# ScalarE in pairs of banks with one VectorE tile beside, accumulators drawn from the free banks, a multiply moved to GpSimd, a late choice of shift engine

## The chip, the cores and the metric

One core of one Trainium2 chip runs the whole program. The metric is the device time of one execution in microseconds (us), taken in several rounds on one chip beside the kernel before. The ratios below use runs not over 1.5% above the fastest run of the same kernel. The engines are TensorE (PE; its weight loads are PEld), ScalarE (ACT), VectorE (DVE), GpSimd (POOL) and the DMA queue of SyncE (SP).

Each run also reports the mean clock granted to TensorE, as a share of full speed.

## The reference

Two independent blocks work on 2048 rows of 512 numbers; their outputs lie side by side.

```python
def _A_ref(x, wq, wk, wv, wo):            # 32 query heads of 16, one key and value head
    q = (x @ wq)...                       # [1, 32, 2048, 16]
    k, v = x @ wk, x @ wv
    scores = einsum("bhqd,bkd->bhqk", q, k) * (Dh ** -0.5)
    p = _softmax(scores, axis=-1)         # 32 x 2048 x 2048 exponentials
    o = einsum("bhqk,bkd->bhqd", p, v)
    return o... @ wo

def _B_ref(x, wqkv, w_phi, wo):           # linear attention, softmax features
    ...                                   # little work beside A
```

Block A's 134 million exponentials are the bulk of the work. Block B is some projections, 64 exponentials of 128 x 512 and many small steps, woven in between.

## The kernel before: the parts that matter

**Tiles and units.** Scores are made in tiles of 128 keys by 512 queries, 2048 of them. They are grouped in 32 accumulators ("sc"), each of 64 tiles, that is 16 quads of four tiles (one for each of TensorE's four row strips). A score tile fills one PSUM bank; the kernel lays PSUM out as eight banks of 128 x 512. A quad goes one of two ways:

- *ScalarE's way:* exponentiate from PSUM into a ring in SBUF, two or three banks per instruction; then TensorE multiplies by the values (`pv`, one turn for the quad).
- *VectorE's way:* turn the scores into the bit pattern of an approximate exponential (`dz`, one instruction a tile), make three shifted copies of the quad in SBUF (`dS`, on VectorE or POOL), and sum four weighted versions on TensorE (`dpv`, four turns for the quad).

**Banks before.** Five banks serve ScalarE (three and two, in turn), bank 5 is the accumulator, banks 6 and 7 serve everything else: VectorE's score tiles, all projections and all of block B.

```python
self.ACC = 5
self.free = [6, 7]
...
def next_qk(self, i):
    us = []
    for _ in range(3 if i % 2 == 0 else 2):
        u = self.take()
        ...
    n0, b0 = self.nu, 0 if i % 2 == 0 else 3
```

**One accumulator.** The next accumulator may not begin until the copy of the last one has been put in VectorE's queue:

```python
def acc_ok(self, sc):
    return self.acc_sc == sc              # set to None at an accumulator's end,
                                          # to sc + 1 when its copy is issued
```

**The finish of an accumulator** is a copy out of PSUM (`ac`), DMAs that spread the denominators, and a multiply of two SBUF tiles of 128 x 512 (`on`), all on VectorE except for the DMAs:

```python
self.add("dve", lambda v: v.tensor_tensor(out=o, in0=accS[:, r, :], in1=R[:, r, :], op=ALU.mult), ...)
```

**A planner orders everything.** While the kernel is built, a greedy planner keeps a clock for each engine from estimated durations, asks which jobs are ready, and issues the most urgent one. What it fixes is the order of each engine's instructions and how many tiles take VectorE's way. `LOCK` names the VectorE jobs that it never places beside a POOL instruction. It also puts in dummy matmuls ("fills") where its plan has TensorE idle for long; they are meant to keep TensorE's clock up.

## Time and profile before

| | kernel before |
|---|---|
| median of 4 runs | 747.89 us (747.03 to 748.63) |
| ScalarE tiles / VectorE tiles | 1512 / 536 |
| busy in the profiled run: ScalarE, VectorE, POOL | 724.5, 663.8, 371.7 us of 748.5 |
| shifts on VectorE / POOL | 219 / 183 |

The profiled run is not one of these four: it took 750.37 us. These are lines of the page of the kernel before: the span, the busy time of each engine (with its share of the span and its instructions), the lines of the chain that ended last, and the costliest groups. A group's columns are line, engine, operation, output and input with shapes, count; then busy us and mean ns; then the engine's idle time just before these instructions and what ended it.

```profile
span 748.5 us, 17531 instructions
PE 717.5 (96%) x7364; PEld 229.7 (31%) x7364; DVE 663.8 (89%) x1104; ACT 724.5 (97%) x676; POOL 371.7 (50%) x262
...
ACT 53%; PE 34%; DVE 10%; DMA 1%; issue 1%; ACTq 0%; DVEq 0%
...
L1641 ACT ACTIVATE f_PT<-f_ps 128x1536 bf16<-128x1536 f32 x605 | 696.4, 1298 | 14.2 <-PE f_ps L1586 13.1
L1769 POOL TENSOR_TENSOR f_Z<-f_Z,f_step 128x1024 int32<-128x1024 int32 x183 | 346.1, 1891 | 334.3 <-DVE f_Z L1764 329.1
L1738 DVE TENSOR_SCALAR f_Z<-f_ps 128x512 int16<-128x512 f32 x536 | 349.4, 681 | 36.3 <-PE f_ps L1586 33.9
L1586 PE MATMUL f_ps<-f_QA,f_KR 32*128 32x512 bf16 x2048 | 316.5, 386 | 17.3 <-ACT f_PT L1641 6.6
...
L1764 DVE TENSOR_SCALAR f_Z<-f_Z 128x2048 int16<-128x2048 int16 x219 | 149.2, 701 | 0.6
...
L1405 PE MATMUL f_ps<-f_ones,f_zero 128*32 128x512 bf16 (+8 forms) x264 | 49.2, 375 | 1.9 <-POOL f_zero L1424 1.3
```

How to read it. ScalarE is busy 97% and its exponentials (the first group) are the largest share of the chain: the time is, nearly, ScalarE's work. TensorE's 96% says less: 49.2 us are fills (the last line), and the Trainium skill ("Perfetto Trace Analysis", Identifying the Most-Contended Engine) warns that matmul busy time does not tell how close TensorE is to its limit. VectorE's tiles (`f_Z<-f_ps`) waited 33.9 us for a score matmul.

The same kernel's groups with shapes kept apart show the two widths and the multiply:

```profile
L1641 ACT ACTIVATE f_PT<-f_ps 128x1536 bf16<-128x1536 f32 x302 | 455.9, 1509 | 13.0 <-PE f_ps L1586 12.3
L1641 ACT ACTIVATE f_PT<-f_ps 128x1024 bf16<-128x1024 f32 x303 | 329.2, 1087 | 1.2 <-PE f_ps L1586 0.8
...
L1874 DVE TENSOR_TENSOR f_On<-f_accS,f_denS 128x512 bf16<-128x512 f32 x16 | 12.8, 797 | 4.3 <-DMA f_denS<-f_denS 4.3
...
L1874 DVE TENSOR_TENSOR f_Ot<-f_accS,f_denS 128x512 bf16<-128x512 f32 x15 | 10.6, 708 | 0.0
```

The means (1509, 1087 ns) overlap one another, so the price is read from start to start in the trace: 1.330 us for three banks when nothing delays the next, 0.904 us for two. I call a start that comes over 25 ns later than that *late*; before, 94 starts are late, by 20.0 us together.

### The profile page before, as it was taken

Reading aid. Unit: us, or ns where it says so; the run is one execution under the profiler, and the core shown is the slowest. Engines: PE = TensorE matmul, PEld = TensorE weight load, DVE = VectorE, ACT = ScalarE, POOL = GpSimd, SP = SyncE. Lnnn points to the kernel's source line nnn. Section 1 sums busy time; section 2 is a strip of 40 time slices with the busy share of each in tenths; the row PEclk is TensorE's granted clock in tenths of the full one; section 3 lists DMA queues with packets and bytes.
Section 4 is the critical chain, followed back from the end, with each engine's and each line's share of the span. In section 5 each row is a group of like instructions: output and inputs, shape, how many; then the busy total and the mean of one; then the engine's idle time right before and its main releaser. Section 6 shows DMA issues by size and latency. Waiting matters only on the chain.

```text
span 748.5 us, 17531 instructions
## 1 busy us (share of the span) xinstructions
PE 717.5 (96%) x7364; PEld 229.7 (31%) x7364; DVE 663.8 (89%) x1104; ACT 724.5 (97%) x676; POOL 371.7 (50%) x262
## 2 busy tenths in 40 slices
PE   8999999999999999989999999999999999999995
PEld 3323233233322323322232333233333333323321
DVE  4999998998998999998869999889998897999992
ACT  5999999999999999998999999999999999999995
POOL 4344466556555554345564454446545754553452
PEclk9999999999999999999999999999999999999999
DMA  6521223111102111011101112101111111111112
GB/s 142 115 37 8 37 36 75 9 11 10 10 6 36 12 9 9 7 8 9 12 4 10 29 23 27 9 2 27 19 16 9 23 33 26 16 9 20 19 16 40
DMA packets 47887, 18.25 MB, mean 24 GB/s; under 512 B 38708, under 2 KB 45940, under 8 KB 47800
## 3 DMA queue, kind: packets, MB, share of 16 engines
q1 hardware_dynamic: 45400, 16.23, 16.7%
q8 instruction: 59, 0.97, 0.5%
q10 hardware_dynamic: 2400, 0.82, 0.5%
q14 instruction: 28, 0.23, 0.1%
HBM read 2.28 MB, written 4.19 MB: 9 GB/s over the span
## 4 chain that ended last, share of the span: by engine, by line
ACT 53%; PE 34%; DVE 10%; DMA 1%; issue 1%; ACTq 0%; DVEq 0%
ACT f_PT L1641 51%; PE f_ps L1586 12%; PE f_ps L1806 9%; PE f_ps L1682 5%; DVE f_Z L1738 4%; ACT f_Ek L2059 2%; DVE f_Z L1764 2%; PE f_ps L2241 1%; PE f_ps L1405 1%; PE f_ps L1893 1%; PE f_ps L2149 1%; ACT f_ET L2156 1%; PE f_ps L1576 1%; DMA f_AxT<-in_A_x_dram 1%; PE f_ps L2225 1%
## 5 line engine op out<-in xcount | busy, mean ns | idle before, releaser
L1641 ACT ACTIVATE f_PT<-f_ps 128x1536 bf16<-128x1536 f32 x605 | 696.4, 1298 | 14.2 <-PE f_ps L1586 13.1
L1769 POOL TENSOR_TENSOR f_Z<-f_Z,f_step 128x1024 int32<-128x1024 int32 x183 | 346.1, 1891 | 334.3 <-DVE f_Z L1764 329.1
L1738 DVE TENSOR_SCALAR f_Z<-f_ps 128x512 int16<-128x512 f32 x536 | 349.4, 681 | 36.3 <-PE f_ps L1586 33.9
L1586 PE MATMUL f_ps<-f_QA,f_KR 32*128 32x512 bf16 x2048 | 316.5, 386 | 17.3 <-ACT f_PT L1641 6.6
L1806 PE MATMUL f_ps<-f_Z,f_VK 128*32 128x512 f16 x2144 | 189.7, 389 | 3.0 <-DVE f_accS L1411 1.3
L1586 PEld LDWEIGHTS f_ps<-f_QA,f_KR 32*128 32x128 bf16 x2048 | 82.2, 91 | 249.2 <-ACT f_PT L1641 133.1
L1764 DVE TENSOR_SCALAR f_Z<-f_Z 128x2048 int16<-128x2048 int16 x219 | 149.2, 701 | 0.6
L1682 PE MATMUL f_ps<-f_PT,f_VA 128*32 128x512 bf16 x1512 | 149.3, 388 | 0.2
L1806 PEld LDWEIGHTS f_ps<-f_Z,f_VK 128*32 128x32 bf16 x2144 | 48.6, 94 | 97.5 <-issue 62.6
L1682 PEld LDWEIGHTS f_ps<-f_PT,f_VA 128*32 128x32 bf16 x1512 | 38.6, 94 | 69.1 <-issue 62.7
L1405 PE MATMUL f_ps<-f_ones,f_zero 128*32 128x512 bf16 (+8 forms) x264 | 49.2, 375 | 1.9 <-POOL f_zero L1424 1.3
L2211 DVE TENSOR_TENSOR f_Wk<-f_ps,f_wq 128x512 bf16<-128x512 f32 x32 | 21.9, 685 | 2.5 <-PE f_ps L2200 2.3
L2065 DVE TENSOR_REDUCE f_ssum<-f_Ek 128x64 f32<-128x1024 bf16 x16 | 19.4, 1215 | 2.5 <-ACT f_Ek L2059 2.5
L1411 DVE COPY f_accS<-f_ps 128x512 f32<-128x512 f32 x31 | 21.1, 681 | 0.6 <-PE f_ps L1682 0.6
L1405 PEld LDWEIGHTS f_ps<-f_ones,f_zero 128*32 128x32 bf16 (+2 forms) x264 | 13.4, 98 | 24.2 <-issue 17.3
L2099 DVE TENSOR_TENSOR f_vS<-f_ps,f_rs 128x1024 bf16<-128x1024 f32 x16 | 19.5, 1221 | 1.4 <-PE f_ps L2089 1.3
L2156 ACT ACTIVATE f_ET<-f_ps 128x512 bf16<-128x512 f32 x32 | 19.1, 709 | 0.0
L2059 ACT ACTIVATE f_Ek<-f_ps 128x512 bf16<-128x512 f32 x32 | 18.7, 682 | 0.0
L2051 PE MATMUL f_ps<-f_Wk,f_BxT 128*128 128x512 bf16 x64 | 16.6, 382 | 0.0
L2241 PE MATMUL f_ps<-f_Bwo,f_oT 128*128 128x512 bf16 x64 | 16.6, 382 | 0.0
L2089 PE MATMUL f_ps<-f_Bwv,f_BxT 128*128 128x512 bf16 x64 | 16.6, 382 | 0.0
L2149 PE MATMUL f_ps<-f_BxT,f_Wq 128*128 128x512 bf16 x64 | 16.6, 381 | 0.0
(96 smaller groups left out, 302.8 us busy)
## 6 DMA issues: line engine op xcount, KB each, us to landing
f_denS<-f_denS SPq DMA_DIRECT2D x124, 30.0 KB, 3.1
out_dram<-f_outB SPq DMA_DIRECT2D x16, 128.0 KB, 2.7
f_denC<-f_accS SPq DMA_DIRECT2D x124, 2.0 KB, 1.7
f_denS<-f_denC SPq DMA_DIRECT2D x124, 2.0 KB, 1.7
out_dram<-f_outA SPq DMA_DIRECT2D x14, 128.0 KB, 2.3
f_On<-f_Ot SPq DMA_DIRECT2D x60, 16.0 KB, 1.8
f_Bwv<-in_B_wqkv_dram SPq DMA_DIRECT2D x1, 512.0 KB, 5.1
f_Bwo<-in_B_wo_dram SPq DMA_DIRECT2D x1, 512.0 KB, 4.4
```

The lines of the kernel that those rows point to most:

```text
L1405: mm = pe.matmul(ps[m * i:m * i + m, bank, 0:n].rearrange("p (a n) -> p a n", n=128), lhsT=zero[0:r, 0:m], rhs=rhs, start=start, stop=star ...
L1586: return pe.matmul(self.ps[:, bank, :], lhsT=self.KR[32 * g:32 * g + 32, sc % 2, kap * 128:(kap + 1) * 128], rhs=self.QA[32 * g:32 * g + 3 ...
L1641: self.add("act", lambda a: a.activation(out=PT[:, sl[0]:sl[0] + size, :], in_=ps[:, b0:b0 + size, :], func=ACT.Exp), reads=[("PS", b0 + i ...
L1682: mm = pe.matmul(ps[32 * g:32 * g + 32, bank, :], lhsT=VA[:, kap, :], rhs=PT[:, slots[g], :], start=start, stop=stop, tile_position=(0, 32 ...
L1738: self.add("dve", lambda v: v.tensor_scalar(out=o, in0=ps[:, bank, :], scalar1=self.Z1, scalar2=self.Z0, op0=ALU.mult, op1=ALU.add), reads ...
L1764: fn = lambda v: v.tensor_scalar(out=Z[:, z], in0=Z[:, z0], scalar1=256.0 * t, scalar2=None, op0=ALU.add)
L1769: fn = lambda g: g.tensor_tensor(out=b, in0=a, in1=c, op=ALU.add)
L1806: mm = pe.matmul(ps[32 * g:32 * g + 32, bank, :], lhsT=self.VK[:, t, kap, :], rhs=Zf[:, sl[g], :], start=start, stop=stop, tile_position=( ...
L2059: self.add("act", (lambda a, sg: (lambda e: e.activation(out=Ek[:, r, a, :, :], in_=ps[:, bank, :].rearrange("p (h f) -> p h f", h=32), fu ...
L2149: mm = pe.matmul(ps[:, bank, :], lhsT=w[:, dc, G * 128:G * 128 + 128], rhs=xT[:, dc, m * 512:(m + 1) * 512], start=(dc == 0), stop=(dc == 3))
L2156: self.add("act", lambda e: e.activation(out=self.ET[:, sl, :], in_=self.ps[:, bank, :], func=ACT.Exp, scale=1.0 - 2.0 * a), reads=[("PS", ...
L2241: mm = pe.matmul(ps[:, bank, :], lhsT=oT[:, r, C, :], rhs=self.Bwo[:, C, :], start=(C == 0), stop=(C == 3))
```

## The change

The intent: give ScalarE regular pairs (four banks), so that a bank is freed; put one VectorE tile beside a pair in the same TensorE turn; draw accumulators from the free banks, so that the next can open while the last is still copied or unfinished; take the multiply off VectorE; choose the engine of a quad's second and third shift late, when it is known how far POOL is. Several constants of the planner move with it.

```diff
-        self.ACC = 5
-        self.free = [6, 7]
+        self.ACC = 4
+        self.free = [4, 5, 6, 7]
...
-        for _ in range(3 if i % 2 == 0 else 2):
+        for _ in range(2):
...
-        n0, b0 = self.nu, 0 if i % 2 == 0 else 3
+        n0, b0 = self.nu, 0 if i % 2 == 0 else 2
... (a VectorE score tile only in a row-mode turn, one at a time)
     def dq_ok(self):
         if self.dbusy > self.DBUSY or self.dz_out >= self.NOUT:
             return False
+        if self.mode != "row" or self.beside:
+            return False
... (accumulators)
-        return self.acc_sc == sc
+        return sc == self.acc_sc or (sc == self.acc_sc + 1 and (("acc", sc) in self.bk or first))
...
+            self.bk[acc] = [min(self.free, key=lambda b: (self.tr.get(("PS", b), (0.0,))[0], b))]
... (the multiply)
-            job(("on", sc), "dve", 0.60, ...
+            job(("on", sc), "pool", 1.16, ...
-    LOCK = ("dS", "on", "qw")
+    LOCK = ("dS", "qw")
... (the shifts: t=1 on VectorE; when it is done, t=2 and 3)
+                if t == 1:
+                    rest()
+        def rest():
+            for t in (2, 3):
+                left = max(self.te["pool"] - self.fin, 0.0) + self.PSHIFT * self.pooled
+                spare = 1.84 * (16 - self.at[sc] - self.dt[sc]) + (30 if sc > self.asc else 0)
+                job(t, "pool" if left < self.PLEFT[t - 2] and left + self.PSHIFT < spare + self.CLOSE else "dve")
...
-    AHEAD = 6
+    AHEAD = 5
-    HIGH = 13
+    HIGH = 16
```

More of the change, by code (lines that the diff above doesn't have):

```diff
@@ L1251, in __init__ @@
         self.tile_end, self.row_free, self.row_next = [0.0] * 4, 0.0, set()
-        self.open = False
         self.held = 0
+        self.beside = False
     TAIL = dict(pe=0.17, act=0.10, dve=0.09, pool=0.1)
@@ L1315, in ready @@
                     t = max(t, f)
-        if j.nb:
+        nb = j.nb or (1 if self.acc_of(j) else 0)
+        if nb:
             fr = sorted(max(self.tr.get(("PS", b), (0.0,))[0], 0.0) + self.SEM for b in self.free)
-            if len(fr) < j.nb:
+            if len(fr) < nb:
                 return None
-            t = max(t, fr[j.nb - 1])
+            t = max(t, fr[nb - 1])
         return t
@@ L1334, in issue @@
                 self.tile_end[x] = start + dur
+        if j.eng == "pe":
+            self.beside = j.name[0] == "dq"
         self.te[j.eng] = max(self.te[j.eng], start + dur)
@@ L1345, in issue @@
             self.held += j.name[0] != "dq"
+        acc = self.acc_of(j)
+        if acc:
+            self.bk[acc] = [min(self.free, key=lambda b: (self.tr.get(("PS", b), (0.0,))[0], b))]
+            self.free.remove(self.bk[acc][0])
         j.fn()
@@ L1348, in issue @@
             self.free += self.bk[f]
-            self.held -= f[0] != "dq"
+            self.held -= f[0] not in ("dq", "acc")
         self.issued.add(j.name)
@@ L1519, in jobs_a @@
             job(("rc", sc), "dve", 0.16, (lambda sc: (lambda: self.finish_sc2(sc)))(sc), after=[("ac", sc)], prio=1.1)
-            job(("on", sc), "dve", 0.60, (lambda sc: (lambda: self.finish_sc3(sc)))(sc), prio=1.3,
+            job(("on", sc), "pool", 1.16, (lambda sc: (lambda: self.finish_sc3(sc)))(sc), prio=1.3,
                 after=[("rc", sc)] + ([("op", 4 * ((sc - 12) // 8) + i) for i in range(4)] if sc >= 12 and sc % 2 == 0 else []) + ([("on", sc - 1)] if sc % 2 else []))
@@ L1653, in expo, with acc_ok, acc_of, opened @@
                              ok=(lambda sc: (lambda: self.acc_ok(sc)))(self.aquads[q][0]))
-    def acc_ok(self, sc):
-        return self.acc_sc == sc
+    def acc_ok(self, sc, first=True):
+        return sc == self.acc_sc or (sc == self.acc_sc + 1 and (("acc", sc) in self.bk or first))
+    def acc_of(self, j):
+        sc = self.aquads[j.name[1]][0] if j.name[0] == "pv" else self.dquads[j.name[1]][0] if j.name[0] == "dpv" else None
+        return None if sc is None or ("acc", sc) in self.bk else ("acc", sc)
+    def opened(self):
+        return next((self.bk["acc", sc][0] for sc in (self.acc_sc, self.acc_sc + 1) if sc < 32 and 0 < self.ndone[sc] < 64), None)
     def sums(self, sc, n):
@@ L1663, in sums @@
             self.ndone[sc] += n
-            self.open = not stop
             if stop:
-                self.acc_sc = None
+                self.acc_sc = sc + 1
                 if sc < 31:
-                    self.job(("ac", sc), "dve", 0.60, lambda: self.finish_sc(sc), prio=0, after=[("on", sc - 2)] if sc >= 2 else [])
+                    self.job(("ac", sc), "dve", 0.60, lambda: self.finish_sc(sc), prio=0, after=[("on", sc - 2)] if sc >= 2 else [], frees=[("acc", sc)])
         return start, stop
@@ L1676, in pv @@
         start, stop = self.sums(sc, 4)
-        bank = self.ACC
+        bank = self.bank(("acc", sc))
         def fn(pe):
@@ L1774, in go, with job @@
                 self.zused(quad)
+                if t == 1:
+                    rest()
             return go
         ok = lambda: len(self.zfree) > (quad > self.zold)
-        who, own = {}, []
-        for t in (3, 2, 1):
-            left = max(self.te["pool"] - self.fin, 0.0) + self.PSHIFT * self.pooled
-            eng = "pool" if t > 1 and left < self.PLEFT[3 - t] else "dve"
+        own = []
+        def job(t, eng):
             if eng == "pool":
@@ L1784, in shifts @@
                 self.dbusy += 0.6
-            who[t] = eng
-        for t in (1, 2, 3):
-            eng = who[t]
-            self.job(("dS", quad, t), eng, 0.60 if eng == "dve" else self.PSHIFT, shift(t, eng), prio=2 if eng == "dve" else 1 + t, ok=ok,
-                     after=[("dS", quad, x) for x in range(1, t) if who[x] == "dve"] if eng == "pool" else [])
+            self.job(("dS", quad, t), eng, 0.60 if eng == "dve" else self.PSHIFT, shift(t, eng), prio=(self.OWN if t == 1 else 2) if eng == "dve" else 1 + t, ok=ok,
+                     after=[("dS", quad, 1)] if t > 1 else [])
+        def rest():
[3 more added lines that the diff above has]
+                job(t, "pool" if left < self.PLEFT[t - 2] and left + self.PSHIFT < spare + self.CLOSE else "dve")
+        job(1, "dve")
         for t in range(4):
             self.job(("dpv", quad, t), "pe", 0.218, (lambda t: (lambda: self.d_pv(quad, t)))(t), mode="col", prio=1.4,
-                     after=([("dS", quad, t)] if t else []) + [("va", x) for x in range(4)], ok=lambda: self.acc_ok(sc))
+                     after=([("dS", quad, t)] if t else []) + [("va", x) for x in range(4)], ok=lambda: self.acc_ok(sc, False))
     def d_pv(self, quad, t):
@@ L1800, in d_pv @@
         start, stop = self.sums(sc, 1)
-        bank = self.ACC
+        bank = self.bank(("acc", sc))
         def fn(pe):
@@ L1825, in finish_sc @@
         accS, denC = self.accS, self.denC
-        self.copy(accS[:, r, :], ps[:, self.ACC, :], [("PS", self.ACC)], [("accS", r)])
+        bank = self.bank(("acc", sc))
+        self.copy(accS[:, r, :], ps[:, bank if bank is not None else 0, :], [("PS", bank)], [("accS", r)])
         fs = []
@@ L1832, in finish_sc @@
         self.dmas(fs, [("accS", r)], [("denC", r)], 0.6)
-        if self.rec is None:
-            self.acc_sc = sc + 1
     def finish_sc2(self, sc):
@@ L1873, in finish_sc3 @@
         o, key = (self.Ot[:, p % 2, :], ("Ot", p % 2)) if r else (self.On[:, p % 6, :], ("On", p % 6))
-        self.add("dve", lambda v: v.tensor_tensor(out=o, in0=accS[:, r, :], in1=R[:, r, :], op=ALU.mult),
+        self.add("pool", lambda v: v.tensor_tensor(out=o, in0=accS[:, r, :], in1=R[:, r, :], op=ALU.mult),
                  reads=[("accS", r), ("denS", r), ("row", r)], writes=[key])
@@ L1921, in finish_last @@
     def finish_last(self):
-        ps, lnd, part, oa, ACC = self.ps, self.lnd, self.part, self.outA, self.ACC
+        ps, lnd, part, oa, ACC = self.ps, self.lnd, self.part, self.outA, self.bank(("acc", 31))
         H = 256
@@ L2253 @@
     PSHIFT = 1.97
-    PLEFT = (4.0, 2.0, 0.0)
-    LOCK = ("dS", "on", "qw")
+    PLEFT = (4.0, 2.0)
+    LOCK = ("dS", "qw")
     NEAR = 0.15
@@ L2270 @@
     LEFT = 8
-    AHEAD = 6
+    AHEAD = 5
     AGE = 3.0
     AGED = 0.8
-    HIGH = 13
+    HIGH = 16
     DBUSY = 3.0
     NOUT = 2
+    CLOSE = 0
+    OWN = 1.1
     T_B = (54.0, 600.0)
@@ L2330, in run @@
                 s, j = next((p for p in picks if p[1].eng == "pool" and p[1].asked <= s + self.NEAR and self.te_port <= s + self.NEAR), (s, j))
-            bank = self.ACC if self.open else next((b for b in self.free if self.tr.get(("PS", b), (0.0,))[0] + self.SEM <= self.te["pe"]), None)
+            at = self.opened()
+            bank = at if at is not None else next((b for b in self.free if self.tr.get(("PS", b), (0.0,))[0] + self.SEM <= self.te["pe"]), None)
             if j.eng == "pe" and bank is not None and self.force(j, s, bank):
@@ L2340, in run @@
                     cols = [512] * (n // 4) + ([128 * (n % 4)] if n % 4 else [])
-                    self.issue(_Job(("fill", len(self.log)), "pe", 0.0533 * n, lambda: self.fill(cols, start=not self.open, mode=m, bank=bank), (), m, 0, (), 0, 9, None), te)
+                    self.issue(_Job(("fill", len(self.log)), "pe", 0.0533 * n, lambda: self.fill(cols, start=at is None, mode=m, bank=bank), (), m, 0, (), 0, 9, None), te)
                     continue
@@ L2348, in force @@
     def force(self, j, s, bank):
-        te = self.te["pe"]
+        te, at = self.te["pe"], self.opened()
         end = s + j.dur + (self.SWITCH[j.mode] if j.mode != self.mode else 0)
@@ L2359, in force @@
         n = self.FORCE
-        self.issue(_Job(("fill", len(self.log)), "pe", 0.2133 * n / 512, lambda: self.fill([n], start=not self.open, mode=m, bank=bank), (), m, 0, (), 0, 9, None), te)
+        self.issue(_Job(("fill", len(self.log)), "pe", 0.2133 * n / 512, lambda: self.fill([n], start=at is None, mode=m, bank=bank), (), m, 0, (), 0, 9, None), te)
         return True
     def gather(self, opts):
-        if self.mode == "col" or self.acc_sc is None or self.acc_sc > 30:
+        if self.mode == "col" or self.acc_sc > 30:
             return opts
@@ L2379, in rank @@
         if j.eng == "pe":
-            if j.name[0] == "pv" and self.nu - 4 * self.pvq > self.HIGH:
+            if j.name[0] in ("pv", "dpv") and self.nu - 4 * self.pvq > self.HIGH:
                 p = 0.5
```

## The prediction

> **What bounds the kernel now.** 2048 score tiles (128 keys by 512 queries) are split between two engines: ScalarE exponentiates 1512 of them (302 instructions of three banks, 303 of two), VectorE approximates 536 by integer arithmetic (134 quads of four). The page has ScalarE busy 97%, and in the hundreds from 100 to 700 us (windows view) 97 to 100%; VectorE 87 to 95% there, POOL 44 to 59%. TensorE reads 96%, but 49 us of that are dummy fills, so it has slack. The chain of waits is 51% exponentials. The time is ScalarE's work: 696 us of exponentials (0.4606 us a tile) + 38 us of other activations + about 14 us of start, tail and waits. Only fewer ScalarE tiles, or cheaper ones, shorten it.
>
> **ScalarE's price per tile.** Start to start in the trace, an undelayed three-bank instruction takes 1.330 us (0.443 a tile), a two-bank one 0.904 (0.452). 94 starts come late, 20 us together, 12 of them beside full-array projections. All pairs undelayed cost +0.005 a tile, +8 us over 1500 tiles. There will be some 745 instructions instead of 605, and each must be refilled in a 0.904 us window, never 1.330. I estimate delays of 20 to 30 us. So ScalarE costs 0.465 to 0.471 a tile: 7 to 15 us worse.
>
> **What it buys.** (a) The normalising multiply moves to POOL: 31 instructions, 23.4 us (by-form groups) off VectorE. POOL will take about 1.06 us each (estimate from its 1.891 us for 1024 columns against 0.401 for 128), 33 us of its 334 idle. (b) One bank freed: three or two instead of two to draw from, and a second open accumulator. That removes a pause at each change of accumulator and part of VectorE's 34 us of waiting for its score matmul. (c) The late choice of shift engine should send more shifts to POOL: now 183 of 402, I expect 45 to 52%. (d) The VectorE tile rides beside a pair: TensorE row tiles run together (Trainium skill, "TensorE: Matmul & The Clock Gate", Part 3); the trace agrees, three score matmuls start and end within 0.39 us.
>
> A quad costs VectorE 4 x 0.652 + 1.63 x 0.681 = 3.7 us and saves ScalarE 1.84. Freed VectorE time of 23 us plus about 20 us of idle removed plus some 12 us of shifts sent to POOL, shared with the shortening itself, gives 9 to 12 more quads: 143 to 146, or 16 to 22 us less ScalarE work. The removed pauses give ScalarE perhaps 3 us more.
>
> **Sum.** 748 - 19 - 3 + 11 = 737 us, about 1.4% faster.
>
> **What the profile should show.** ScalarE exponentials all of two banks, 730 to 745 of them, start to start 0.904 when undelayed, mean 0.93 to 0.945. 570 to 585 VectorE tiles instead of 536. No multiply into On/Ot on VectorE; 31 on POOL near 1.06 us. VectorE 91 to 94% in the middle; POOL 57 to 62%. Fewer dummy fills, since there are more row-mode sessions (632 runs of score matmuls now, above 700 then).
>
> **What would make it wrong.** Pairs never delayed (0.452 a tile, minus 20 us) with the same VectorE gain would pass 2%. The reverse: delays growing with TensorE's crowded windows, or VectorE starved because at most one of its tiles goes beside each pair, would make it a draw.
>
> Faster by over 2%: 0.32; within 2%: 0.62; slower: 0.06. Range 725 to 748.

## The result, and the profile after

The median went from 747.89 to **734.70 us** (734.31 to 735.65, 4 runs each). The ratio is 0.9826, 95% interval 0.9809 to 0.9843: the mean time of the changed kernel's fast runs over that of the other's of the same rounds, so not quite the ratio of the medians. This is clear of the noise, but under 2%.

The page of the changed kernel, the lines that answer to those above:

```profile
span 733.8 us, 18010 instructions
PE 699.0 (95%) x7480; PEld 219.4 (30%) x7480; DVE 681.2 (93%) x1136; ACT 711.6 (97%) x801; POOL 466.2 (64%) x321
...
ACT 47%; PE 32%; DVE 16%; DMA 1%; issue 1%; POOL 1%; SPq 1%; POOLq 0%; ACTq 0%; DVEq 0%
...
L1648 ACT ACTIVATE f_PT<-f_ps 128x1024 bf16<-128x1024 f32 x730 | 683.2, 1075 | 11.4 <-PE f_ps L1593 9.9
L1784 POOL TENSOR_TENSOR f_Z<-f_Z,f_step 128x1024 int32<-128x1024 int32 x211 | 399.8, 1895 | 198.6 <-DVE f_Z L1779 190.4
L1753 DVE TENSOR_SCALAR f_Z<-f_ps 128x512 int16<-128x512 f32 x588 | 379.1, 679 | 21.7 <-PE f_ps L1593 19.5
...
L1779 DVE TENSOR_SCALAR f_Z<-f_Z 128x2048 int16<-128x2048 int16 x230 | 161.7, 728 | 1.1 <-POOL f_Z L1784 0.3
...
L1893 POOL TENSOR_TENSOR f_On<-f_accS,f_denS 128x512 bf16<-128x512 f32 x16 | 20.9, 1305 | 25.6 <-DMA f_denS<-f_denS 24.3
L1412 PE MATMUL f_ps<-f_ones,f_zero 128*32 128x256 bf16 (+6 forms) x224 | 35.6, 347 | 1.3 <-POOL f_zero L1431 1.3
```

ScalarE still sets the time, at the same 97%. It has 1460 tiles instead of 1512. Its price per tile rose from 696.4 / 1512 = 0.4606 to 683.2 / 1460 = 0.4679 us. VectorE took 588 tiles instead of 536, and waits less for them (19.5 us instead of 33.9).

The fall of the profiled span, 748.5 to 733.8 us, splits into:

| term | us |
|---|---|
| 52 ScalarE tiles fewer, at 0.4606 | -24.0 |
| dearer tiles: 1460 x (0.4679 - 0.4606) | +10.7 |
| everything that is not an exponential (52.1, now 50.6) | -1.5 |
| sum (the spans differ by 14.7) | -14.8 |

The two profiled runs had different granted clocks, 0.992 and 0.998. At the slopes given next that is worth 3 to 4 us of the 14.7, so the terms hold for these two runs and not for equal clock.

TensorE's clock is a covariate. The runs of the *kernel before* on three chips, the same program each time, differ almost wholly with it. On one chip: 746.64 us at a granted 0.998, 747.82 at 0.996, 751.71 at 0.992, 754.04 at 0.987. A straight line fitted to each chip's fast runs leaves 0.3 to 0.5 us and has a slope of 0.53 to 0.73 us per 0.001 of clock. So experiments are compared below at equal granted clock too. At 0.998 the kernel before takes 746.6 to 747.9 us, and the changed one 734.3 to 735.7: about 12 of the 13 us are the change itself. (A program may also lower its own clock, as e5 below suggests; a comparison at equal clock then takes away a part of its effect.)

### The profile page after: what moved, and what is told of

The parts are those of the page before. It is cut to its first block, busy times and chain, and to the rows that moved or that the text cites. A ratio compares the mean times of both kernels' runs of the same rounds, so it can differ in the third digit from the quotient of the medians.

```text
span 733.8 us, 18010 instructions
## 1 busy us (share of the span) xinstructions
PE 699.0 (95%) x7480; PEld 219.4 (30%) x7480; DVE 681.2 (93%) x1136; ACT 711.6 (97%) x801; POOL 466.2 (64%) x321
## 4 chain that ended last, share of the span: by engine, by line
ACT 47%; PE 32%; DVE 16%; DMA 1%; issue 1%; POOL 1%; SPq 1%; POOLq 0%; ACTq 0%; DVEq 0%
ACT f_PT L1648 45%; PE f_ps L1593 11%; PE f_ps L1826 7%; DVE f_Z L1753 7%; DVE f_Z L1779 5%; PE f_ps L1695 3%; PE f_ps L1412 1%; DMA f_denC<-f_accS 1%; PE f_ps L2260 1%; PE f_ps L1583 1%; PE f_ps L2168 1%; PE f_ps L2108 1%; ACT f_ET L2175 1%; ACT f_Ek L2078 1%; PE f_ps L2070 1%
## 5 line engine op out<-in xcount | busy, mean ns | idle before, releaser
L1648 ACT ACTIVATE f_PT<-f_ps 128x1024 bf16<-128x1024 f32 x730 | 683.2, 1075 | 11.4 <-PE f_ps L1593 9.9
L1784 POOL TENSOR_TENSOR f_Z<-f_Z,f_step 128x1024 int32<-128x1024 int32 x211 | 399.8, 1895 | 198.6 <-DVE f_Z L1779 190.4
L1753 DVE TENSOR_SCALAR f_Z<-f_ps 128x512 int16<-128x512 f32 x588 | 379.1, 679 | 21.7 <-PE f_ps L1593 19.5
L1593 PE MATMUL f_ps<-f_QA,f_KR 32*128 32x512 bf16 x2048 | 299.8, 384 | 17.2 <-ACT f_PT L1648 12.2
L1826 PE MATMUL f_ps<-f_Z,f_VK 128*32 128x512 f16 x2352 | 211.7, 387 | 6.9 <-DVE f_Z L1779 2.5
L1779 DVE TENSOR_SCALAR f_Z<-f_Z 128x2048 int16<-128x2048 int16 x230 | 161.7, 728 | 1.1 <-POOL f_Z L1784 0.3
L1695 PE MATMUL f_ps<-f_PT,f_VA 128*32 128x512 bf16 x1460 | 138.2, 385 | 0.1
L1695 PEld LDWEIGHTS f_ps<-f_PT,f_VA 128*32 128x32 bf16 x1460 | 36.0, 94 | 51.4 <-issue 44.7
L1893 POOL TENSOR_TENSOR f_On<-f_accS,f_denS 128x512 bf16<-128x512 f32 x16 | 20.9, 1305 | 25.6 <-DMA f_denS<-f_denS 24.3
L1412 PE MATMUL f_ps<-f_ones,f_zero 128*32 128x256 bf16 (+6 forms) x224 | 35.6, 347 | 1.3 <-POOL f_zero L1431 1.3
L1893 POOL TENSOR_TENSOR f_Ot<-f_accS,f_denS 128x512 bf16<-128x512 f32 x15 | 19.6, 1304 | 16.4 <-DMA f_denS<-f_denS 14.8
```

What stands on the lines that cost most here:

```text
L1412: mm = pe.matmul(ps[m * i:m * i + m, bank, 0:n].rearrange("p (a n) -> p a n", n=128), lhsT=zero[0:r, 0:m], rhs=rhs, start=start, stop=star ...
L1593: return pe.matmul(self.ps[:, bank, :], lhsT=self.KR[32 * g:32 * g + 32, sc % 2, kap * 128:(kap + 1) * 128], rhs=self.QA[32 * g:32 * g + 3 ...
L1648: self.add("act", lambda a: a.activation(out=PT[:, sl[0]:sl[0] + size, :], in_=ps[:, b0:b0 + size, :], func=ACT.Exp), reads=[("PS", b0 + i ...
L1695: mm = pe.matmul(ps[32 * g:32 * g + 32, bank, :], lhsT=VA[:, kap, :], rhs=PT[:, slots[g], :], start=start, stop=stop, tile_position=(0, 32 ...
L1753: self.add("dve", lambda v: v.tensor_scalar(out=o, in0=ps[:, bank, :], scalar1=self.Z1, scalar2=self.Z0, op0=ALU.mult, op1=ALU.add), reads ...
L1779: fn = lambda v: v.tensor_scalar(out=Z[:, z], in0=Z[:, z0], scalar1=256.0 * t, scalar2=None, op0=ALU.add)
```

## The experiments

Theory A is the accounting in my prediction: VectorE is short of *time*; every microsecond taken off it becomes tiles. Theory B: in the kernel before, VectorE is short of *score tiles at the right moment* (banks and TensorE's turns); time off VectorE is worth something only once it is fed. Twelve kernels ran; all computed correct results. After each edit the planner makes a new order of the whole program, so that no run changes one thing alone.

The results together. "At its clock" is one run, with its granted clock, and beside it what the kernel before or after took at that clock (in part on another chip; none where no such run exists):

| run | median | ratio to before | at its clock |
|---|---|---|---|
| changed kernel | 734.70 | 0.983 | 734.42 at 0.997 |
| e1 multiply alone | 751.57 | 1.003 | 749.17 at 0.995; before 749.56 and 749.83 |
| e2 multiply back | 788.82 | 1.054 | 785.68 at 0.985 |
| e3 multiply back, urgent | 737.52 | 0.984 | 735.95 at 0.997; after 734.42 |
| e4 multiply back, beside POOL | 756.18 | 1.008 | 756.75 at 0.987; before 754.04 |
| e5 pairs alone | 765.20 | 1.022 | 763.40 at 0.977 |
| e12 pairs and multiply | 744.71 | 0.993 | 743.54 at 0.996; before 748.17 |
| e10 pairs, multiply, beside | 738.78 | 0.980 | 733.93 and 735.87 at 0.997; after 734.42 |
| e6 three and two again | 766.64 | 1.027 | 765.67 at 0.991; before 752.53 |
| e7 one open accumulator | 750.93 | 1.003 | 748.51 at 0.996; after 734.98 |
| e8 no rule "beside" | 783.20 | 1.045 | 780.22 at 0.984 |
| e9 early choice | 738.60 | 0.986 | 735.81 at 0.997; after 734.42 |
| e11 constants set anew | 741.65 | 0.989 | 740.52 at 0.998; after 734.31 and 735.65 |

The medians of e10 and e11 each include one slow run (745.02 and 752.58 us), the ratios do not.

### e1: the multiply alone

```diff
 (kernel before)
-            job(("on", sc), "dve", 0.60, ...        self.add("dve", ... tensor_tensor ...
+            job(("on", sc), "pool", 1.16, ...       self.add("pool", ... tensor_tensor ...
-    LOCK = ("dS", "on", "qw")
+    LOCK = ("dS", "qw")
```

> The kernel before, with only the normalising multiply moved from VectorE to POOL. Theory A (my prediction's term a): VectorE time is what limits the number of its tiles, so 23.4 us freed are worth about 4 quads, 8 us: 740 us. Theory B: VectorE in the kernel before is short of score tiles at the right moment (banks, TensorE's rhythm), not of time; the freed time becomes idle time: 746 to 750 us. As built, the program still gives ScalarE 1512 tiles, which speaks for B; the chip decides the time. Either way the multiply on POOL should take about 1.3 us as in the changed kernel.

Measured: 751.57 us, ratio 1.0028 (0.9971 to 1.0085): the same. The program has the same 1512 ScalarE tiles. The line of VectorE's tiles shows that it is no better fed:

```profile
L1738 DVE TENSOR_SCALAR f_Z<-f_ps 128x512 int16<-128x512 f32 x536 | 348.5, 682 | 38.7 <-PE f_ps L1586 36.4
```

VectorE waits for score matmuls as before (36.4 us; 33.9 before). Theory A's term is refuted for this kernel: 23.4 us of VectorE time bought nothing. Some 9 us more of VectorE's span are idle (93.8 us, 84.7 before), and some 10 went into its shifts (159.7 us busy, 149.2 before): 13 of them took over 0.9 us, where the median is 0.68, each behind a POOL instruction that had started first (6 such before).

### e2, e3, e4: the multiply back on VectorE in the changed kernel

```diff
 (changed kernel; e2)
-            job(("on", sc), "pool", 1.16, ... prio=1.3
+            job(("on", sc), "dve", 0.60, ... prio=1.3      LOCK with "on"
 (e3: the same with prio=0.5)    (e4: as e2, but LOCK without "on")
```

e2 deadlocked at first, since each engine waits for a flag before its last instructions and these counts (80 on TensorE, 8 on ScalarE) no longer fitted the new order; it ran with shorter counts (8 and 6), and so did e8 and e12.

> The changed kernel with the multiply back on VectorE, as in the kernel before (lowest urgency of its kind, never beside a POOL instruction). As built it has 1500 ScalarE tiles instead of 1460. By the price per tile (0.468 us, plus 50.6 us that are not exponentials) theory A says 753 us. Theory B adds: the multiply is starved by the busier POOL, it comes tens of us after its accumulator copy and holds the accumulators and the end of the program, so 760 to 790 us. The reservations of the last instructions for the check of the flag were shortened, or the program would deadlock; that alone should cost under 2 us.

> The changed kernel with the multiply back on VectorE, but urgent there (priority 0.5 instead of 1.3). As built: 1464 ScalarE tiles. Theory A: VectorE loses 23 us, so 743 us. Theory B: the multiply's engine is worth little once it is not starved: 1464 x 0.468 + 50.6 = 736 us, 735 to 739.

> The changed kernel with the multiply back on VectorE and allowed beside POOL instructions. As built: 1460 ScalarE tiles. If VectorE and POOL do not hinder one another in such work, the multiply stays near 0.75 us and the time is 733 to 737 us. If they do, the multiply's mean, or that of POOL's shifts at its side, is far above 0.75 and 1.90 us, and the time is 3 to 15 us above 735.

Measured: 788.8, 737.5 and 756.2 us.

- e2: the multiply seldom finds a moment without POOL in time. From an accumulator's copy to its multiply it takes 41 us in the median and 75 at most (17 and 21 in the changed kernel). The end of the program is then a long tail: the last exponential starts at 738.8 us, but the span is 783.9, and block B's last output copy starts at 762.4. The flag comes only at 771.0 (652.3 in the changed kernel), and TensorE stands still 9.4 us for it; how much of the tail is the flag's, no run separates.
- e3: made urgent, it costs 1 to 3 us at equal clock. So 21.5 us of VectorE time are worth little in the changed kernel too, *as long as the multiply is not starved*. Theory A had 8 us.
- e4: here the planner puts the multiply beside POOL, with the same 1460 tiles as the changed kernel, and the hardware disagrees. Of this kernel's timeline, the VectorE and POOL pieces around one multiply (start, us, engine, line):

```profile
286.38 2.47 DVE L1753 TENSOR_SCALAR f_Z<-f_ps 128x512 int16<-128x512 f32 x4
286.54 3.86 POOL L1784 TENSOR_TENSOR f_Z<-f_Z,f_step 128x1024 int32<-128x1024 int32 x2 [6.73 <-DVE f_Z L1779]
...
288.78 2.17 DVE L1893 TENSOR_TENSOR f_On<-f_accS,f_denS 128x512 bf16<-128x512 f32 x1
```

And around another, which starts before POOL's two shifts do:

```profile
330.31 0.69 DVE L1893 TENSOR_TENSOR f_On<-f_accS,f_denS 128x512 bf16<-128x512 f32 x1
...
330.47 4.25 POOL L1784 TENSOR_TENSOR f_Z<-f_Z,f_step 128x1024 int32<-128x1024 int32 x2 [4.45 <-DVE f_Z L1779]
```

The first multiply takes 2.17 us and ends 0.55 us after POOL's second shift (286.54 + 3.86 = 290.40). In e3, where POOL is kept away, 29 of 31 multiplies take 0.675 to 0.693 us. In e4 the mean is 1.29 us. All 25 multiplies that start while a shift runs end 0.546 to 0.550 us after that shift, however long it still had to run. The reverse holds too: all 11 shifts that start while a multiply runs end 1.749 to 1.753 us after the multiply, and take 2.22 to 2.27 us instead of 1.89. So this multiply and POOL's shift exclude one another, and the one that starts second stands still. POOL pays less in all (mean 1.913 us; 1.895 in the changed kernel) because it is seldom second. (VectorE's shifts meet POOL in the same way: those of over 0.9 us, 13 in e1 and 23 in e11, all end 0.55 us after the POOL instruction that they met.) The Trainium skill ("GPSIMD Engine Reference", Specifications) lists this contention, for "DVE instructions in a 2-port perf mode or with two SBUF inputs"; the trace agrees and adds its size. The delays were not in the plan, so ScalarE's late starts rose from 19 to 37.7 us (some 10 of these in or within 1 us of half-clock intervals, of which the changed kernel's profile has none before its last microseconds). Granted clock fell as well (0.989 at best), and at equal clock e4 is no better than the kernel before.

So the multiply's move to POOL removes an instruction that excludes POOL; it does not mainly buy VectorE time.

### e5 and e12: pairs alone, then with the multiply

```diff
 (kernel before; e5)
-        self.ACC = 5                              -  range(3 if i % 2 == 0 else 2)    -  0 if i % 2 == 0 else 3
-        self.free = [6, 7]                        +  range(2)                         +  0 if i % 2 == 0 else 2
+        self.ACC = 4
+        self.free = [5, 6, 7]
 (e12: the same and the edit of e1; shorter counts for the flag, as in e2)
```

> The kernel before with pairs alone: two banks per ScalarE instruction, and the bank so freed given to the pool of free banks (three); one fixed accumulator, multiply on VectorE, early choice of shift engine. As built: 1472 ScalarE tiles, but 295 of 432 shifts on VectorE. If the pairs and their bank are the gain, the price per tile says 1472 x 0.468 + 51 = 740 us. If VectorE's time is then the limit (more tiles, more shifts and still the multiply), ScalarE must wait for VectorE's share at each accumulator's end: 748 to 755 us, with VectorE above 93% and POOL below 45%.

> Pairs alone (765 us) with the multiply moved to POOL, nothing else of the change. As built: 1456 ScalarE tiles, 300 of 444 shifts on VectorE. If the multiply's 23 us are what VectorE lacked once pairs feed it well, 738 to 748 us, a gain of about 20 us where the same move alone gave nothing to the kernel before. If VectorE is still overfull, it stays at 755 to 768 us and the part B output comes late again. (Reservations of the last instructions shortened.)

Measured: 765.2 us, 2.2% slower than before (1.7 to 2.7%), and 744.7 us, the same as before: 20 us less once the multiply is moved, the move that gave nothing by itself. Part of that difference is clock: 763.4 us at 0.977 against 743.5 at 0.996, and at the fitted slopes those 0.019 are 10 to 14 us, which leaves 6 to 10. Likewise, the lines of the kernel before give 758 to 763 us at 0.977 (762.8 on e5's own chip, extended from runs at 0.991 and above): at equal clock e5 is 1 to 5 us slower than before. The two lines that follow are VectorE's tiles in e5 and a wait of TensorE (who, for whom, us in total, times, longest), to which I come back:

```profile
L1738 DVE TENSOR_SCALAR f_Z<-f_ps 128x512 int16<-128x512 f32 x576 | 361.8, 677 | 5.6 <-PE f_ps L1586 5.4
...
PE f_ps L2200 <- DVE flag L1977: 2.7, 1, 2.7
```

e5's half-clock time lies mostly in the last stretch, as the windows view of e5 shows (columns: stretch, its length, busy us and instructions of PE, PEld, DVE, ACT, POOL, granted clock, DMA share, GB/s):

```profile
50.00:350.00 300.00, 292.17 (x3030) 89.92 (x3051) 298.61 (x496) 299.18 (x336) 122.44 (x82) 1.00 0.17 20
350.00:650.00 300.00, 292.79 (x2973) 95.24 (x2989) 291.94 (x492) 295.76 (x337) 114.71 (x78) 0.99 0.14 15
650.00:700.00 50.00, 49.40 (x491) 17.18 (x492) 49.65 (x83) 49.68 (x57) 16.78 (x10) 1.00 0.15 21
700.00:712.00 12.00, 11.28 (x127) 3.80 (x120) 11.10 (x25) 11.96 (x14) 3.46 (x2) 1.00 0.22 24
712.00:737.00 25.00, 22.82 (x147) 5.89 (x147) 16.41 (x27) 15.28 (x16) 6.05 (x3) 0.52 0.10 6
737.00:762.00 25.00, 15.70 (x120) 6.65 (x118) 12.07 (x22) 6.07 (x10) 1.89 (x1) 0.90 0.17 54
```

Until 700 us ScalarE and VectorE are as full as can be. Counting starts in the traces tells what they achieved:

| | tiles of both engines started by 650 us | block B output copies started by 650 us (of 16) | last exponential starts | span |
|---|---|---|---|---|
| before | 1794 | 12 | 736.8 | 748.5 |
| e1 multiply alone | 1791 | 13 | 735.3 | 747.4 |
| e5 pairs alone | 1830 | 5 | 739.4 | 761.9 |
| e12 pairs and multiply | 1852 | 6 | 718.5 | 742.9 |
| changed | 1840 | 13 | 721.0 | 733.8 |

Pairs and the bank that they free do feed VectorE: its wait for score matmuls falls from 33.9 to 5.4 us in e5, and 36 more tiles are started by 650 us. But VectorE then has no time for block B, whose jobs are less urgent to the planner; 11 of its 16 outputs are left for the end, where nothing else is left to fill ScalarE, and TensorE's clock is halved, from 712.9 us for 23.9 us. The half clock began inside a wait for the flag: the flag needs late steps of block B and came at 713.5 us (651.8 in the kernel before), and TensorE stood still for it from 711.4 to 714.1.

With the multiply off VectorE (e12), the last exponential starts 21 us earlier. Not all of that is shown to be the multiply's: e12 also has the shorter counts, and TensorE does not wait for its flag (at 720.0 us), so the half clock of e5's tail may have gone with the counts. No run separates the two. The counts only set where each engine waits for the flag, so the state at 650 us is free of them: there e12 is 22 tiles ahead of e5, which at the rate of both engines (1830 tiles in 640 us) is worth 7.7 us by my estimate. The multiply's 23 us are now worth about the 8 us of theory A. Neither part gains alone: e1 lacks the supply, e5 the time. But the move is not needed for the gain: in e3 the other parts of the change are in place, the multiply is back on VectorE, and it costs only 1 to 3 us.

e12's exponentials end even before those of the changed kernel, and it loses that again in its tail: its last block B output copy starts at 731.1 us, that of the changed kernel at 666.1.

### e10: pairs, multiply and the rule "beside", without the other parts

```diff
 (kernel before, with the edits of e12 but the long counts, AHEAD = 5, HIGH = 16 and)
     def dq_ok(self):
+        if self.mode != "row" or self.beside:
+            return False
```

> The kernel before with pairs, the rule beside, the multiply on POOL and two of the ordering constants; one fixed accumulator and the early choice stay. As built: 1464 ScalarE tiles, 273 shifts on VectorE. Pairs alone were 765 us because VectorE fell behind with its other work; if taking the multiply off VectorE and spacing its tiles cures that, the price per tile says 1464 x 0.468 + 51 = 736 us, 734 to 741. If the floating, doubly open accumulator carries the gain (its removal alone cost 16 us), 745 to 755 us.

Measured: 733.9 and 735.9 us at 0.997, as the changed kernel at that clock (734.4). Its other runs had lower clocks (738.8 at 0.992, 744.4 at 0.982, and a slow one, 745.0 at 0.982), so the median is 738.8; its ratio is 0.9803 (0.9715 to 0.9891). e12's tail is gone: 14 of block B's output copies have started by 650 us instead of 6. I put that down to the spacing of VectorE's tiles, but the two constants changed with it and the counts for the flag are the long ones again; which of them cured the tail is not shown. So, at equal clock, pairs with their bank, the multiply on POOL, the rule "beside" and two constants suffice for the whole gain. (Whether this program draws the lower clocks more often, five runs do not say.) The floating accumulator and the late choice of shift engine add nothing that these runs show.

### e6, e7, e8, e9: one part of the changed kernel undone

```diff
 (e6) range(2) -> range(3 if i % 2 == 0 else 2); free = [5, 6, 7]
 (e7) acc_ok: return sc == self.acc_sc
 (e8) dq_ok without the two new lines; shorter counts for the flag, as in e2
 (e9) rest() called when the four score tiles are done, not after the first shift
```

> The changed kernel with ScalarE's three-and-two banks of before (and so one free bank fewer). As built: 1544 ScalarE tiles, 126 VectorE quads. If the free bank and the regular rhythm do not matter, this is 735 us or better, since a tile costs 0.4606 instead of 0.468 us. If they are what feeds VectorE, 1544 x 0.4606 + 51 = 762 us, slower than before, with VectorE below 85%.

> The changed kernel with one accumulator open at a time (its bank still drawn from the free ones). Tiles as built: 1460 as in the changed kernel. If the second accumulator is worth nothing, 735 us. If ScalarE was kept waiting at the 31 changes of accumulator, some 0.2 us each: 740 to 744 us, with waits of ScalarE of over 1 us at a few of those changes.

> The changed kernel without the rule that a VectorE score tile goes only beside a pair. As built: 1424 ScalarE tiles, 156 VectorE quads. If VectorE's share alone decides, 1424 x 0.468 + 51 = 717 us. If TensorE's rhythm decides, VectorE's tiles issued on their own cost TensorE a turn each and delay ScalarE's pairs: late starts above 30 us and more idle time of ScalarE, 745 to 770 us in spite of fewer tiles. (Reservations of the last instructions shortened as in the run with the multiply back.)

> The changed kernel with the engine of a quad's second and third shifts chosen when its four score tiles are done, not when its first shift is done. As built: 1460 ScalarE tiles as before, but 257 shifts on VectorE instead of 230 (27 x 0.70 = 19 us more VectorE work). If VectorE still has idle time to absorb it, 734 to 738 us with VectorE near 95%. If the kernel as changed is bound by VectorE too, 740 to 750 us.

e6: 766.6 us; 762 had been expected from the price per tile. The wider instructions are cheaper for ScalarE, but VectorE starves with three banks for tiles, accumulators and all the rest. Its tiles' line:

```profile
L1753 DVE TENSOR_SCALAR f_Z<-f_ps 128x512 int16<-128x512 f32 x504 | 338.7, 685 | 102.7 <-PE f_ps L1593 100.3
```

Of 100.3 us, 80.8 are more than in the changed kernel. This is theory B's shortage, shown directly.

e7: 750.9 us with the very same 1460 tiles. ScalarE's late starts are 33.0 us instead of 19.0. Most of its loss shows in these waits of ScalarE (who, for whom, us in total, times, longest), which were 9.9 us in the changed kernel; the second line is new:

```profile
ACT f_PT L1648 <- PE f_ps L1593: 14.2, 21, 6.9
ACT f_PT L1648 <- PE f_ps L1695: 6.6, 5, 1.8
```

ScalarE waits for the multiply by the values (L1695), because its ring of results is full while the next accumulator may not be opened (so the program's order has it; no run took this wait away by itself). Taken alone, e7 says that the second open accumulator is worth 13.5 us. e10, without it, says zero. Both are right of their programs: an undone part leaves the others' constants tuned for its presence, and the planner finds a different order. The part is needed *there*, not for the gain. (A rival for part of e7's loss: VectorE's shifts that take over 0.9 us lose 15.6 us in all against 0.69 each, most of them behind POOL's multiply; in the changed kernel it is 8.6. Whether the closed accumulator brings this about is not shown.)

e8: 783.2 us with the *fewest* ScalarE tiles of all, 1424. The price per tile had said 717. Late starts rise to 44.4 us (19 of them in half-clock intervals, one of which lasts 30.7 us from 103.6 us on; what set it off was not looked into), and ScalarE stands idle in waits that the changed kernel does not have:

```profile
ACT f_ET L1958 <- DVE f_ET L1954: 21.7, 1, 21.7
ACT f_ET L2173 <- PE f_ps L2166: 19.6, 5, 8.5
```

The second line is block B's exponentials waiting for their projections, the first the last step of block A waiting for VectorE, which is behind with block B and computes the flag only at 769.5 us. No block B output was copied by 650 us. The rule "beside" is a throttle on VectorE's tiles as much as a way to make them cheap for TensorE: without it VectorE takes tiles greedily and pays with the tail.

e9: 735.8 us at 0.997, 1.4 us over the changed kernel at that clock; its other runs are mixed with lower clocks. VectorE absorbed the 27 more shifts, with 689 us of busy time instead of 681. The effect is small.

### e11: constants set anew

```diff
-    NEAR = 0.15   URGE = 1.1   MINCOL = 0   QS = 0.9   SLACK = 0.8   LEFT = 8    AHEAD = 5   AGE = 3.0   DBUSY = 3.0
+    NEAR = 0.25   URGE = 1.0   MINCOL = 2   QS = 0.8   SLACK = 0.6   LEFT = 12   AHEAD = 6   AGE = 5.0   DBUSY = 4.0
-    T_B = (54.0, 600.0)
+    T_B = (54.0, 580.0)
```

> The changed kernel with ten of its ordering constants set anew. As built: 1448 ScalarE tiles, 150 quads. Price per tile: 1448 x 0.468 + 51 = 729 us, so 726 to 732 us if the price of a tile holds; 733 to 738 us if the tighter order brings late starts back.

I tried many settings of the constants and kept the one whose planned end, by the planner's own estimated durations, was earliest (5 us earlier than that of the changed kernel). Measured: 740.5 to 741.7 us at 0.998, some 6 us *slower* than the changed kernel at that clock. It has 12 ScalarE tiles fewer (worth 5.6 us), but late starts of 38.0 us instead of 19.0 (some 8 of them in or within 1 us of half-clock intervals of its profiled run, which was at 0.988). My reading, which no run tests, is that the estimates leave no margin for what they do not know, and a tighter order turns each small error into a late start. The trace has one such error: the planner reckons 1.16 us for POOL's multiply, which takes 1.27 in the median, and 17 of VectorE's shifts stand behind it (6 in the changed kernel); the shifts over 0.9 us lose 20.8 us in all, 8.6 in the changed kernel.

## Why the prediction was right or wrong

The time was right: 737 predicted, 734.7 measured. Point by point:

- *The bound.* ScalarE at 97% before and after: right.
- *Price per tile* 0.465 to 0.471 us: right, 0.468. The term was +11 and came to +10.7. Its parts were less right: I expected 20 to 30 us of late starts; there were 19.0, no more than before, though there are 125 more instructions. Two half-clock intervals inside the profiled run before, which the profiled run after does not have, held (counting 1 us around them) 5.3 of the 20.0 us of late starts before; outside them late starts rose from 14.7 to 19.0 us. So the match of +11 and +10.7 is partly luck: without the half clock in the profile before, the term would have been larger, by up to some 5 us (an estimate).
- *Tiles for VectorE:* 9 to 12 more quads; 13 came. The term was -19 and came to -24.0.
- *Term (a), where most of these were to come from,* is the step that failed. I counted 23 us freed on VectorE as time that turns into tiles. Moved alone it gave nothing (e1); moved back with urgency it cost 1 to 3 us (e3). It has some worth, about 8 us by estimate, where pairs feed VectorE and its tiles are not spaced (e5 against e12, with the counts for the flag as a rival for the rest), and as the removal of an instruction that excludes POOL (e2, e4).
- *Term (b), the freed bank,* was right in direction and mis-sized by me as the smaller part. It is what feeds VectorE: waits of 33.9 us before, 5.4 with pairs alone, 19.5 in the changed kernel, 100.3 in it with three-and-two.
- *Term (c), more shifts on POOL:* 48%, inside the 45 to 52% forecast, but undoing the late choice cost only about 1.4 us (e9), and e10 reached the whole gain with 165 of 438 shifts on POOL.
- *Pauses at accumulators,* -3 us: the whole non-exponential remainder fell by 1.5 us.
- *Marks in the profile:* 730 instructions, mean start to start 0.935 us between pairs, 704 runs of score matmuls, fills down from 49.2 to 35.6 us, all as forecast or at the edge. 588 tiles against 585 at most, POOL at 64% against 62 at most, and the multiply on POOL 1.305 us against my estimate of 1.06 were outside. I had scaled the multiply from an integer addition and a small product, each of which repeats one of its inputs; the price of two full 32-bit inputs was in neither, though no run tests that this is the reason. The Trainium skill ("GPSIMD Engine Reference", Engine selection) has POOL about twice as slow for two-input work, and this agrees: 1.305 us on POOL against 0.68 undisturbed on VectorE, 1.9 times.
- *What I said would make it wrong,* VectorE starved because only one tile goes beside each pair, is the opposite of what happened: without that limit the kernel is 48 us slower (e8; at a lower clock, 0.984 at best).

So the sum was right partly by luck: errors of -5.0 on the tiles and +1.5 on the pauses stand against each other, the match on the price leans on the clock of one profile, and the reason that I weighted most for the tiles was the wrong one of two.

What stays open: what each part of the changed kernel is worth in itself. Undoing parts cost 1 to 54 us each, which add to several times the gain; e10 shows that at least two of them are not needed. Between e12 and e10, the rule "beside" and the two constants were not tried apart.

## What to carry to other kernels

When two engines share a pool of work, ask of the second engine whether it lacks time or supply, from what ends its waits, before counting time taken off it as a gain; the two limits can hide each other: here the multiply's move paid nothing before pairs, about 8 us (an estimate) beside pairs alone, and 1 to 3 us with all the rest in place. An engine that takes all the shared work it can get may starve the work that nobody else can do, which then reappears as a tail: look at what is still left at 90% of the span. And compare at equal granted clock: here 0.010 of clock was worth about as much as half of the change.

## What the Trainium skill lacked or had wrong

- "GPSIMD Engine Reference", Specifications and Key points: these two sections name the contention between POOL and a VectorE instruction with two SBUF inputs, without its size or who pays (other pages of the skill treat it further, so this is a gap of the page alone). In e4 it is an exclusion, paid by the one that starts second: the multiply ends 0.55 us after the shift that it met (25 of 25), the shift 1.75 us after the multiply that it met (11 of 11).
- "TensorE: Matmul & The Clock Gate", HAM oscillation: "The abstract rule is 'no PE-idle gaps >~3.4µs.'" Here the clock was halved at 333.6 us in the kernel before although the longest gap between matmuls in the 7 us before it was 0.57 us; TensorE had been busy 5.57 of the 6.80 us before. The page's next section does describe an oscillation by small gaps, without a figure for how many it takes. The lengths of the intervals inside the profiled runs, such as 3.413, 6.827 and 10.24 us, are multiples of the page's window.
- The same page does not say what throttled time costs a kernel whose limit is another engine than TensorE. Here it is 0.53 to 0.73 us per 0.001 of mean granted clock, of about 750 us, from runs of one program.
- Outside the start of a kernel, no page read says that the granted clock of one program varies from run to run on one core alone: 0.980 to 0.998 for the kernel before in the fast runs on one chip.
